# Second layer norm of a transformer block: statistics at the residual sum, rows read back in exchanged 32-blocks and turned by VectorE

## The chip, the cores and the metric

The kernel runs on one core of a Trainium2 chip. The metric is the device time of one execution in microseconds, given as the median of several runs. Engines are named as the profile names them: PE is TensorE (PEld its weight loads), DVE is VectorE, ACT is ScalarE, POOL is GpSimd, SP is SyncE, which here only issues DMA transfers.

## The reference

One block over 2048 tokens of 1024 features, in float32: layer norm, linear attention with a learned feature map (32 heads of 32), residual; then layer norm, an MLP with relu (1024 to 3584 to 1024), residual.

```python
def _layernorm(x, eps=1e-5):
    m, v = mean(x, -1), var(x, -1)
    return (x - m) / sqrt(v + eps)

# attention: q, k, v = x @ wqkv, per head
phi_q = concat(softmax(q @ w_phi), softmax(-(q @ w_phi)));  phi_k likewise
o = phi_q @ (phi_k.T @ v) / (phi_q @ phi_k.sum(0) + 1e-6)
h = x + attention(layernorm(x)) @ wo
out = h + relu(layernorm(h) @ w1) @ w2
```

The change concerns `layernorm(h)`, the second layer norm. TensorE needs its result with the features on the partitions, while `h` has the tokens there.

## The kernel before

There are 16 row tiles of 128 tokens (`NT`, half of them `HT` = 8). Every float32 product is made of three products of split operands (`mm3`, lines 181 to 183): a rounded high part and the remainder. A split is a cast on ScalarE (L124 for weights) and a subtraction on VectorE or GpSimd (L128).

The stages follow each other on TensorE: projections to keys, values and queries; attention and its output projection (`wo`) interleaved, tile group by tile group; the up projection; the down projection. Up and down are products of 2x2 blocks by seven multiplications (Winograd's form of Strassen), so the normalised rows are needed as seven sums of blocks, `hs[b, m]`, for each half `b` of the tokens.

The order is written out by hand. `items` is the list of pieces of TensorE work; each item of 8 steps (4 in the up projection) has three matmuls a step. `when(step, f, ...)` hangs other work behind a step. The instructions of each engine are issued in that order, and each engine works through its own queue in order. Steps below are counted in this unit. The class `Units` loads weight tiles (`raw`, six buffers) and splits them into a ring of ten (`w`), as soon as a place is free and the step allows. All its loads go through SP's queue, as do nearly all other transfers.

The path of the second layer norm before the change:

- `wo_load` (L645) reads the tile of x, `wo_add` (L671) adds it to the projection in PSUM on VectorE, `wo_store` (L674) writes the sum to DRAM as `hd[t]`.
- `ln_pair(b, i, stage)` takes two row tiles, one of each half of the rows of `b`: stage 0 reads both back (L214, 512 KB each), stage 1 takes statistics on VectorE (L220, L222), stage 2 makes scale and shift on GpSimd (L229 to L231), stage 3 normalises on ScalarE (L237, 128x1024), stages 4 to 6 turn three halves by TensorE (four transposes each into a PSUM bank, L244) and evict them on ScalarE (L246), stage 7 turns the last half (L701; for `b` = 0 evicted by ScalarE, L703) and forms two sums on VectorE (L705, L706), stage 8 forms two more on GpSimd (L711, L712).
- `ln_store` (L721) writes the seven blocks to `hs`, `h_load` (L729) reads them for the up projection, `h_high` and `h_low` (L737, L741) split them.

`LN2` gives the steps of the stages. The four pairs of `b` = 0 run beside attention and `wo`, 40 steps apart; the four of `b` = 1 run beside the up projection of `b` = 0, 68 steps apart. Beside the first run the attention steps of unit `u`: `at_load` (L530, a read of 512 KB through SP), `at_sums` (L562, GpSimd), `at_reduce`, `at_den`, `at_inverse`, `at_scale` (L600, GpSimd), `at_turn` (L606, VectorE, turns 32x32 blocks in place) and `at_num` (L620, TensorE), whose banks are evicted to `oT` by ScalarE (L627) and VectorE (L638). The up projection's blocks are evicted by `up_take` (L764) and the other functions of `UP_BESIDE`.

Of the kernel before, what the change touches and what calls it, by code (L numbers as in the profile page):

```python
# [15 lines left out]
P = 128  # L16
# [123 lines left out]
def kernel(  # L140
# [56 lines left out]
    hd = [dram.tile([P, D], F32, name=f"hd{t}") for t in range(NT)]  # L197

# [26 lines left out]
    def ln_power(key):  # L225

        mv = xst[key]
        sc = scx[:, key[1] - HT, :] if key[0] == "s" else lnp.tile([P, 2], F32, name="sc", bufs=4)
        pool.tensor_scalar_add(sc[:, 0:1], mv[:, 1:2], LN_EPS)  # L229
        pool.tensor_tensor(out=sc[:, 0:1], in0=sc[:, 0:1], in1=half, op=ALU.pow)  # L230
        pool.tensor_scalar(sc[:, 1:2], mv[:, 0:1], sc[:, 0:1], -1.0, op0=ALU.mult, op1=ALU.mult)  # L231
        xst[key] = sc

    def ln_norm(key):
        sc, src = xst.pop(("s", key[1]) if key[0] == "x" and key[1] >= HT else key), xin.pop(key)
        xnt[key] = src if key[0] == "h" else fp_ln.tile([P, D], F32, name="xn")
        act.activation(xnt[key], src, AF.Identity, bias=sc[:, 1:2], scale=sc[:, 0:1])  # L237

    def ln_turn(key, j, dst=None):
# [5 lines left out]
        if dst is None:  # L245
            act.activation(xn[:, j * 512:(j + 1) * 512], pt.rearrange("p k n -> p (k n)"), AF.Copy)  # L246
            return
# [430 lines left out]

    def ln_pair(b, i, stage):

        keys = [("h", HT * b + 4 * r + i) for r in range(2)]
        if stage == 0:
            for key in keys:
                ln_load(key, [hd[key[1]]])
        elif stage == 1:
            for key in keys:
                ln_stats(key)
        elif stage == 2:
            for key in keys:
                ln_power(key)  # L690
        elif stage == 3:
            for key in keys:
                ln_norm(key)
        elif stage in (4, 5, 6):
            ln_turn(keys[stage // 6], stage != 4)
        elif stage == 7:
            x1, x2 = (xnt[key] for key in keys)
            s12 = (mp or hp).tile([P, 2, 512], F32, name="s12", bufs=1)
            pt = tp_bank()
            for k in range(4):  # L700
                pe.transpose(pt[:, k * P:(k + 1) * P], x2[:, k * P:(k + 1) * P], ident)  # L701
            if b == 0:
                act.activation(s12[:, 1, :], pt, AF.Copy)  # L703
                pt = s12[:, 1, :]
            v.tensor_add(s12[:, 0, :], pt, x2[:, 512:])  # L705
            v.tensor_sub(x2[:, 0:512], x1[:, 0:512], pt)  # L706
            sums[b, i] = s12
        elif stage == 8:
            x1, s12 = xnt[keys[0]], sums[b, i]
            s4 = (mp or hp).tile([P, 512], F32, name="s4l", bufs=1)  # L710
            pool.tensor_tensor(out=s12[:, 1, :], in0=s12[:, 0, :], in1=x1[:, 0:512], op=ALU.subtract)  # L711
            pool.tensor_tensor(out=s4, in0=x1[:, 512:], in1=s12[:, 1, :], op=ALU.subtract)  # L712
            sums[b, i] = s12, s4
# [322 lines left out]
    for (t, hf), n in order:  # L1036
        do(max(n - 1, wo_first), -1, wo_load, t, hf)
        when(8 * n + (11 if n < wo_first + 2 else 9), wo_add, t, hf)
# [4 lines left out]
    LN2 = ((0, 9, 12, 17, 24, 25, 26, 27, 29, 36), (0, 18, 26, 32, 40, 42, 44, 46, 50, 60))  # L1043
    wo0 = 8 * wo_first
    up0 = 8 * first_up
    for i in range(4):
        for stage in range(9):
            when(wo0 + 64 + 40 * i + LN2[0][stage], ln_pair, 0, i, stage)
            when(up0 + 60 + 68 * i + LN2[1][stage], ln_pair, 1, i, stage)
        for j in range(7):  # L1050
            when(wo0 + 64 + 40 * i + LN2[0][9] + j // 2, ln_store, 0, i, j)
            when(up0 + 60 + 68 * i + LN2[1][9] + j, ln_store, 1, i, j)
# [56 lines left out]
    scx = consts.tile([P, HT, 2], F32, name="scx")  # L1109
    consts.tile([P, 48], F32, name="fill")  # L1110
# [94 lines left out]
```

## Time and profile before

| | before |
|---|---|
| median of 3 runs | 1911.11 us (1909.57 to 1911.47) |
| span of the profiled execution | 1907.8 us |
| the profiled execution's own time | not listed apart from the runs; its span is 3.3 us below their median |
| VectorE busy | 1034.8 us (54%) |
| ScalarE busy | 758.0 us (40%) |
| GpSimd busy | 974.2 us (51%) |
| granted TensorE clock | 0.999 |
| DMA | 432.14 MB, mean 227 GB/s |

A row of groups gives line, engine, operation, tiles, shapes and count, then the busy time in us and the mean duration in ns, then the idle time of the engine just before and what ended it. A row of the timeline gives start, length, engine and line. A row of a table by stretches gives the bounds in us, the length, then the busy time of PE, PEld, DVE, ACT and POOL with the instructions, the granted clock, the DMA share and GB/s. A row of DMA issues gives the count, the size, and the median time from issue to landing in us.

### The profile page before, as it was taken

The page shows a single profiled execution, that of the slowest core. Times are in us where ns is not written, and L with a number is a line of the kernel's source. Part 1 is how long each engine was busy: PE and PEld are TensorE (multiplying, and loading weights), DVE is VectorE, ACT ScalarE, POOL GpSimd, SP SyncE. Part 2 cuts the span into 40 slices and gives each one's busy share as a digit, 9 for nine tenths or more (in the row PEclk, how much of TensorE's full clock was granted, in tenths as well). Part 3 has the DMA queues.
Part 4 walks back from the last instruction along what each step waited for, and adds up shares of the span by engine and source line. Part 5 has one row for each costly group of instructions (what it writes and reads, how often), then busy time and mean ns, then how long its engine had stood idle before and what let it go on. Part 6 is the DMA issues. An engine that isn't in the chain of part 4 may idle for free.

```text
span 1907.8 us, 31460 instructions
## 1 busy us (share of the span) xinstructions
PE 1894.3 (99%) x11416; PEld 1561.0 (82%) x11416; DVE 1034.8 (54%) x1657; ACT 758.0 (40%) x1314; POOL 974.2 (51%) x961
## 2 busy tenths in 40 slices
PE   9999999999999999999999999999999999999999
PEld 7888888877878888878888888888888888888887
DVE  6666578767679876545644564344433433343333
ACT  5433326222223222245445564444444444444442
POOL 4777752789955988523333222222244444444443
PEclk9999999999999999999999999999999999999999
DMA  6888786666665667796786897566677677767775
GB/s 225 274 267 269 233 273 196 212 192 210 201 196 195 216 206 242 216 303 219 256 252 229 276 294 220 175 195 191 205 255 222 192 239 234 240 212 221 215 215 177
DMA packets 292699, 432.14 MB, mean 227 GB/s; under 512 B 24384, under 2 KB 150336, under 8 KB 292544
## 3 DMA queue, kind: packets, MB, share of 16 engines
q1 hardware_dynamic: 275648, 413.36, 68.5%
q10 hardware_dynamic: 16896, 16.78, 2.6%
q8 instruction: 89, 1.46, 0.3%
q14 instruction: 66, 0.54, 0.1%
HBM read 292.68 MB, written 137.36 MB: 225 GB/s over the span
## 4 chain that ended last, share of the span: by engine, by line
PE 88%; POOL 5%; DMA 4%; issue 1%; DVE 1%; SPq 1%; ACT 0%; POOLq 0%; DVEq 0%; ACTq 0%
PE mm L181 22%; PE mm L182 22%; PE mm L183 22%; PE ac L181 4%; PE ac L182 4%; PE ac L183 4%; PE tp L182 2%; PE tp L183 2%; PE tp L181 2%; POOL b L350 2%; POOL w L128 2%; PE tp L244 1%; PE tp L278 1%; DMA b<-in_w_dram 1%; DMA t<-b 1%
## 5 line engine op out<-in xcount | busy, mean ns | idle before, releaser
L128 POOL TENSOR_TENSOR w<-raw,w 128x512 fp32r<-128x512 f32 x355 | 474.5, 1338 | 725.6 <-ACT w L124 683.2
L124 ACT ACTIVATE w<-raw 128x512 fp32r<-128x512 f32 x686 | 409.3, 626 | 510.8 <-PE mm L183 247.4
L128 DVE TENSOR_TENSOR w<-raw,w 128x512 fp32r<-128x512 f32 x331 | 270.3, 817 | 531.1 <-ACT w L124 527.9
L181 PE MATMUL mm<-w,xT 128*128 128x512 f32 x768 | 311.9, 406 | 0.0
L182 PE MATMUL mm<-w,xT 128*128 128x512 f32 x768 | 301.0, 392 | 3.3 <-POOL w L128 2.9
L183 PE MATMUL mm<-w,xT 128*128 128x512 f32 x768 | 300.6, 391 | 0.0
L182 PE MATMUL mm<-hT,w 128*128 128x512 f32 x672 | 261.7, 389 | 1.3 <-DVE hT L741 1.3
L181 PE MATMUL mm<-hT,w 128*128 128x512 f32 x672 | 262.7, 391 | 0.0
L183 PE MATMUL mm<-hT,w 128*128 128x512 f32 x672 | 261.7, 389 | 0.0
L350 POOL TENSOR_TENSOR b<-b 128x256 f32<-128x256 f32 x224 | 181.9, 812 | 89.7 <-DMA b<-in_w_dram 74.2
L182 PEld LDWEIGHTS mm<-w,xT 128*128 128x128 f32 x768 | 145.0, 189 | 33.6 <-POOL w L128 5.1
L181 PEld LDWEIGHTS mm<-w,xT 128*128 128x128 f32 x768 | 144.9, 189 | 30.8 <-issue 1.7
L183 PEld LDWEIGHTS mm<-w,xT 128*128 128x128 f32 x768 | 144.5, 188 | 30.9
L183 PE MATMUL mm<-w 128*128 128x512 f32 x392 | 152.6, 389 | 0.0
L182 PE MATMUL mm<-w 128*128 128x512 f32 x392 | 152.6, 389 | 0.0
L181 PE MATMUL mm<-w 128*128 128x512 f32 x392 | 152.5, 389 | 0.0
L182 PEld LDWEIGHTS mm<-hT,w 128*128 128x128 f32 x672 | 126.2, 188 | 27.4 <-DVE hT L741 1.7
L183 PEld LDWEIGHTS mm<-hT,w 128*128 128x128 f32 x672 | 126.1, 188 | 26.4
L181 PEld LDWEIGHTS mm<-hT,w 128*128 128x128 f32 x672 | 126.2, 188 | 25.8
L182 PEld LDWEIGHTS mm<-w 128*128 128x128 f32 x392 | 73.6, 188 | 15.3
L183 PEld LDWEIGHTS mm<-w 128*128 128x128 f32 x392 | 73.6, 188 | 15.2
L181 PEld LDWEIGHTS mm<-w 128*128 128x128 f32 x392 | 73.6, 188 | 15.3
(164 smaller groups left out, 3148.6 us busy)
## 6 DMA issues: line engine op xcount, KB each, us to landing
raw<-t SPq DMA_DIRECT2D x224, 256.0 KB, 4.0
raw<-ad SPq DMA_DIRECT2D x196, 256.0 KB, 3.0
raw<-in_w_dram SPq DMA_DIRECT2D x168, 256.0 KB, 3.1
b<-in_w_dram SPq DMA_DIRECT2D x56, 512.0 KB, 4.2
t<-b SPq DMA_DIRECT2D x56, 512.0 KB, 4.2
ad<-c SPq DMA_DIRECT2D x112, 256.0 KB, 3.7
ad<-s SPq DMA_DIRECT2D x84, 256.0 KB, 4.1
ed<-qe ACTq DMA_DIRECT2D x32, 512.0 KB, 4.9
```

The costliest lines, as they stand in the source:

```text
L124: nc.scalar.activation(w[:, 0, :], raw[1], AF.Copy)
L128: eng.tensor_tensor(out=w[:, 1, :], in0=raw[1], in1=w[:, 0, :].bitcast(F32), op=ALU.subtract)
L181: pe.matmul(ps, a_hi, b_hi, start=first, stop=False, skip_group_check=more)
L182: pe.matmul(ps, a_hi, b_lo, start=False, stop=False, skip_group_check=more)
L183: pe.matmul(ps, a_lo, b_hi, start=False, stop=last, skip_group_check=more)
L244: pe.transpose(pt[:, k, :], xn[:, (4 * j + k) * P:(4 * j + k + 1) * P], ident)
L278: pe.matmul(ps[:, i * P:(i + 1) * P], wt_of[p, i][:, k * P:(k + 1) * P], bd[:, (2 * p + i) % 8, :], start=True, stop=True)
L350: pool.tensor_tensor(out=tsum[j, *out], in0=tsum[j, *a], in1=tsum[j, *b], op=ALU.subtract)
```

## The change

The statistics are taken by VectorE right after the residual sum, from the sum in SBUF. GpSimd makes scale and shift there, and SP writes them to a small DRAM array `scd[t]` (8 bytes a row). The tile is read back from `hd` in four transfers (one for each 32 destination partitions), in runs of 32 elements, so that each 32 columns of features come to stand where a 32x32 block turn needs them; with each goes a transfer that reads the scales of the same exchanged rows into `scx`. ScalarE normalises in four passes a tile, one for each group of 32 rows (scale and shift differ between them). VectorE turns the 32x32 blocks in place, and the sums follow from SBUF. TensorE's transposes for this layer norm and their evictions are gone, and the steps in `LN2` are new. The first layer norm keeps its transposes.

```diff
--- before.py
+++ after.py
@@ -195,6 +195,7 @@
     place_of = {t: (b, i) for b, tiles in enumerate(groups) for i, t in enumerate(tiles)}
     ed = [dram.tile([P, 8, 4, 256], F32, name=f"ed{b}") for b in range(4)]
     hd = [dram.tile([P, D], F32, name=f"hd{t}") for t in range(NT)]
+    scd = [dram.tile([P, 2], F32, name=f"scd{t}") for t in range(NT)]
 
 
 
@@ -225,7 +226,7 @@
     def ln_power(key):
 
         mv = xst[key]
-        sc = scx[:, key[1] - HT, :] if key[0] == "s" else lnp.tile([P, 2], F32, name="sc", bufs=4)
+        sc = scx[:, key[1] - HT, 0, :] if key[0] == "s" else lnp.tile([P, 2], F32, name="sc", bufs=4)
         pool.tensor_scalar_add(sc[:, 0:1], mv[:, 1:2], LN_EPS)
         pool.tensor_tensor(out=sc[:, 0:1], in0=sc[:, 0:1], in1=half, op=ALU.pow)
         pool.tensor_scalar(sc[:, 1:2], mv[:, 0:1], sc[:, 0:1], -1.0, op0=ALU.mult, op1=ALU.mult)
@@ -233,18 +234,15 @@
 
     def ln_norm(key):
         sc, src = xst.pop(("s", key[1]) if key[0] == "x" and key[1] >= HT else key), xin.pop(key)
-        xnt[key] = src if key[0] == "h" else fp_ln.tile([P, D], F32, name="xn")
+        xnt[key] = fp_ln.tile([P, D], F32, name="xn")
         act.activation(xnt[key], src, AF.Identity, bias=sc[:, 1:2], scale=sc[:, 0:1])
 
-    def ln_turn(key, j, dst=None):
+    def ln_turn(key, j, dst):
 
         xn = xnt[key]
         pt = tp_bank().rearrange("p (k n) -> p k n", k=4)
         for k in range(4):
             pe.transpose(pt[:, k, :], xn[:, (4 * j + k) * P:(4 * j + k + 1) * P], ident)
-        if dst is None:
-            act.activation(xn[:, j * 512:(j + 1) * 512], pt.rearrange("p k n -> p (k n)"), AF.Copy)
-            return
         d = dst()
         split(d[:, 0, 4 * j:4 * j + 4, :], d[:, 1, 4 * j:4 * j + 4, :], pt)
         if j == 1:
@@ -676,37 +674,46 @@
 
 
 
+    def wo_stats(t, hf):
+        if hf == 0:
+            hst[t] = lnp.tile([P, 2, 6], F32, name="st", bufs=4)
+        v.bn_stats(out=hst[t][:, hf, :], in_=xh[t, hf])
+        if hf == 1:
+            xst["h", t] = mv = lnp.tile([P, 2], F32, name="mv", bufs=4)
+            v.bn_aggr(out=mv, in_=hst.pop(t))
+
+    hst = {}
+
+    def wo_scale(t):
+        sp.dma_start(scd[t], xst.pop(("h", t)))
+
     def ln_pair(b, i, stage):
 
-        keys = [("h", HT * b + 4 * r + i) for r in range(2)]
+        tiles = [HT * b + 4 * r + i for r in range(2)]
         if stage == 0:
-            for key in keys:
-                ln_load(key, [hd[key[1]]])
+            for r, t in enumerate(tiles):
+                xnt["h", t] = x = lnp.tile([P, D], F32, name="xin")
+                for a in range(4):
+                    rows = slice(32 * a, 32 * (a + 1))
+                    sp.dma_start(scx[rows, 2 * i + r], scd[t].rearrange("(g t) s -> t g s", g=4))
+                    sp.dma_start(x[rows].rearrange("p (c g k) -> p c g k", c=8, g=4),
+                                 hd[t].rearrange("(g t) (c a k) -> a t c g k", g=4, a=4, k=32)[a])
         elif stage == 1:
-            for key in keys:
-                ln_stats(key)
-        elif stage == 2:
-            for key in keys:
-                ln_power(key)
-        elif stage == 3:
-            for key in keys:
-                ln_norm(key)
-        elif stage in (4, 5, 6):
-            ln_turn(keys[stage // 6], stage != 4)
-        elif stage == 7:
-            x1, x2 = (xnt[key] for key in keys)
-            s12 = (mp or hp).tile([P, 2, 512], F32, name="s12", bufs=1)
-            pt = tp_bank()
-            for k in range(4):
-                pe.transpose(pt[:, k * P:(k + 1) * P], x2[:, k * P:(k + 1) * P], ident)
-            if b == 0:
-                act.activation(s12[:, 1, :], pt, AF.Copy)
-                pt = s12[:, 1, :]
-            v.tensor_add(s12[:, 0, :], pt, x2[:, 512:])
-            v.tensor_sub(x2[:, 0:512], x1[:, 0:512], pt)
-            sums[b, i] = s12
-        elif stage == 8:
-            x1, s12 = xnt[keys[0]], sums[b, i]
+            for r, t in enumerate(tiles):
+                x = xnt["h", t].rearrange("p (c g k) -> p c g k", c=8, g=4)
+                for g in range(4):
+                    sc = scx[:, 2 * i + r, g]
+                    act.activation(x[:, :, g], x[:, :, g], AF.Identity, bias=sc[:, 1:2], scale=sc[:, 0:1])
+        elif stage in (2, 3):
+            x = xnt["h", tiles[stage - 2]]
+            v.transpose(x, x)
+        elif stage == 4:
+            x1, x2 = (xnt["h", t] for t in tiles)
+            sums[b, i] = s12 = (mp or hp).tile([P, 2, 512], F32, name="s12", bufs=1)
+            v.tensor_add(s12[:, 0, :], x2[:, 0:512], x2[:, 512:])
+            v.tensor_sub(x2[:, 0:512], x1[:, 0:512], x2[:, 0:512])
+        elif stage == 5:
+            x1, s12 = xnt["h", tiles[0]], sums[b, i]
             s4 = (mp or hp).tile([P, 512], F32, name="s4l", bufs=1)
             pool.tensor_tensor(out=s12[:, 1, :], in0=s12[:, 0, :], in1=x1[:, 0:512], op=ALU.subtract)
             pool.tensor_tensor(out=s4, in0=x1[:, 512:], in1=s12[:, 1, :], op=ALU.subtract)
@@ -1035,21 +1042,26 @@
     order = sorted(wo_n.items(), key=lambda kv: kv[1])
     for (t, hf), n in order:
         do(max(n - 1, wo_first), -1, wo_load, t, hf)
-        when(8 * n + (11 if n < wo_first + 2 else 9), wo_add, t, hf)
+        added = 8 * n + (11 if n < wo_first + 2 else 9)
+        when(added, wo_add, t, hf)
+        when(added, wo_stats, t, hf)
+        if hf == 1:
+            when(added + 2, ln_power, ("h", t))
+            when(added + 5, wo_scale, t)
         when(8 * n + (10 if n > order[-3][1] else 14), wo_store, t, hf)
 
 
 
-    LN2 = ((0, 9, 12, 17, 24, 25, 26, 27, 29, 36), (0, 18, 26, 32, 40, 42, 44, 46, 50, 60))
+    LN2 = ((5, 14, 18, 20, 22, 24, 30), (0, 14, 20, 24, 28, 32, 42))
     wo0 = 8 * wo_first
     up0 = 8 * first_up
     for i in range(4):
-        for stage in range(9):
+        for stage in range(6):
             when(wo0 + 64 + 40 * i + LN2[0][stage], ln_pair, 0, i, stage)
             when(up0 + 60 + 68 * i + LN2[1][stage], ln_pair, 1, i, stage)
         for j in range(7):
-            when(wo0 + 64 + 40 * i + LN2[0][9] + j // 2, ln_store, 0, i, j)
-            when(up0 + 60 + 68 * i + LN2[1][9] + j, ln_store, 1, i, j)
+            when(wo0 + 64 + 40 * i + LN2[0][6] + j // 2, ln_store, 0, i, j)
+            when(up0 + 60 + 68 * i + LN2[1][6] + j, ln_store, 1, i, j)
     assert wo_n[8, 0] + 10 < first_up
 
     def up_step(b, p, m):
@@ -1106,8 +1118,7 @@
     eps = consts.tile([P, 1], F32, name="eps")
     pool.memset(eps, DEN_EPS / 2)
     act.activation(consts.tile([P, 1], F32, name="first"), half, AF.Exp)
-    scx = consts.tile([P, HT, 2], F32, name="scx")
-    consts.tile([P, 48], F32, name="fill")
+    scx = consts.tile([P, HT, 4, 2], F32, name="scx")
     wphi = fp.tile([P, 8, 32], F32, name="wphi", bufs=1)
     sp.dma_start(wphi, w_phi.rearrange("(j i) e f -> i e j f", i=4))
     ln_load(("x", 0), [x[0:P, 0:512], x[0:P, 512:1024]])
```

## The prediction

> **What bounds the kernel now.** I read first the page's busy times and the shares of the chain that ended last.
>
> ```profile
> span 1907.8 us, 31460 instructions
> ...
> PE 1894.3 (99%) x11416; PEld 1561.0 (82%) x11416; DVE 1034.8 (54%) x1657; ACT 758.0 (40%) x1314; POOL 974.2 (51%) x961
> ...
> PE 88%; POOL 5%; DMA 4%; issue 1%; DVE 1%; SPq 1%; ACT 0%; POOLq 0%; DVEq 0%; ACTq 0%
> ```
>
> TensorE is busy for 1894.3 of 1907.8 us, so 13.5 us idle is all there is over the whole span. Work taken off TensorE shortens the span unless something makes TensorE wait instead. The median of three runs, 1911.11 us, is 3.3 us above the span of the profiled execution. I sum against the span and add 3.3.
>
> Next come the groups of instructions, for what the change removes, and TensorE's timeline around one pair of row tiles (start, length, engine, line), for what it really costs.
>
> ```profile
> L244 PE MATMUL tp<-ident,xin 128*128 128x128 f32 x96 | 14.4, 273 | 0.0
> L701 PE MATMUL tp<-ident,xin 128*128 128x128 f32 x32 | 4.8, 272 | 0.0
> ```
>
> ```profile
> 692.01 0.39 PE L183 MATMUL mm<-w,oT 128*128 128x512 f32 x1
> 692.24 0.39 PE L181 MATMUL mm<-w,oT 128*128 128x512 f32 x1
> 692.46 0.39 PE L182 MATMUL mm<-w,oT 128*128 128x512 f32 x1
> 692.69 0.39 PE L183 MATMUL mm<-w,oT 128*128 128x512 f32 x1
> 692.92 0.60 PE L244 MATMUL tp<-ident,xin 128*128 128x128 f32 x4
> 693.28 0.48 PE L181 MATMUL mm<-w,oT 128*128 128x512 f32 x1
> 693.59 0.40 PE L182 MATMUL mm<-w,oT 128*128 128x512 f32 x1
> 693.83 0.39 PE L183 MATMUL mm<-w,oT 128*128 128x512 f32 x1
> ...
> 697.21 0.40 PE L183 MATMUL mm<-w,oT 128*128 128x512 f32 x1
> ```
>
> The durations overlap, so neither 273 ns nor the group's busy time is the price. The starts give it. Three matmuls without transposes take 692.69 - 692.01 = 0.68 us, which is one step of the hand-written order. With four transposes among them they take 693.83 - 692.69 = 1.14. From 692.69 to 697.21 lie four such stretches (three of L244, one of L701), 1.13 us each. Four transposes therefore cost 1.13 - 0.68 = 0.45 us.
>
> **The change part by part.**
>
> *TensorE.* Of each of eight pairs 16 transposes go, 96 + 32 = 128 in all, in 32 groups of four: 32 x 0.45 = 14.4 us off an engine that never waits at these places. This is the only large gain. The higher bound would be the groups' busy time, 14.4 + 4.8 = 19.2 us; I take the starts, because the neighbours' overlap is in them.
>
> *ScalarE, VectorE, GpSimd.* ScalarE loses per tile one 128x1024 pass (1.24 us) and per pair three or four 128x512 evictions (0.60 each), and gets eight 128x256 passes (no row of SBUF to SBUF at that size; half of 1.24 at most). So it is no busier. VectorE gets 16 turns of 128x1024 at 1.21 us by the row below, two a pair; its statistics (two of 0.68 us a tile) only move ahead, to behind the residual sum. GpSimd's three small operations a tile move ahead too.
>
> ```profile
> L237 ACT ACTIVATE xin<-xin,sc 128x1024 f32<-128x1024 f32 x16 | 19.5, 1238 | 15.7 <-POOL sc L231 15.4
> L246 ACT ACTIVATE xin<-tp 128x512 f32<-128x512 f32 x24 | 14.4, 598 | 19.9 <-PE tp L244 19.7
> L606 DVE STREAM_TRANSPOSE xin<-xin 128x1024 f32<-128x1024 f32 x4 | 4.8, 1208 | 0.0
> L220 DVE BATCH_NORM_STATS2 st<-xin 128x6 f32<-128x512 f32 x64 | 40.7, 677 | 13.5 <-DMA xin<-in_x_dram 7.9 <-DMA xin<-hd 5.5
> ```
>
> In all VectorE gains 16 x 1.21 = 19.3 us spread over the span, at 54% busy. I cost this at nothing; its cover is that idle half, and if it is gone it shows as attention work late for TensorE (below).
>
> *The read-back.* Two loads of 512 KB a pair become eight of 128 KB in runs of 128 bytes, with eight tiny loads of the scale between them and one tiny store a tile: 16 issues where there were two. Only one transfer of the old kernel has such runs, the first load of all: 128 KB in 1024 runs of 128 bytes.
>
> ```profile
> qe<-ed SPq DMA_DIRECT2D x28, 512.0 KB, 5.4
> ...
> xin<-hd SPq DMA_DIRECT2D x16, 512.0 KB, 5.4
> ...
> wphi<-in_w_phi_dram SPq DMA_DIRECT2D x1, 128.0 KB, 2.5
> ```
>
> ```profile
> 0.72 0.44 SPq L1112 DMA_DIRECT2D wphi<-in_w_phi_dram  x1
> 1.22 1.04 SPq L214 DMA_DIRECT2D xin<-in_x_dram  x2
> ```
>
> ```profile
> 1.80:2.00 0.20, 0.20 (x2) 0.20 (x3) 0.12 (x1) 0.20 (x1) 0.00 (x0) 1.00 0.47 80
> 2.00:2.20 0.20, 0.20 (x3) 0.20 (x3) 0.00 (x0) 0.19 (x1) 0.00 (x0) 1.00 1.08 173
> ```
>
> It lands 2.5 us after its issue, and in the stretch 2.00 to 2.20 us the queues move 173 GB/s (last column), when the next load, issued half a microsecond later, has hardly begun. At 173 GB/s a load of 131 KB takes 0.76 us, and eight take 6.1 us. The other end counts the whole 2.5 us as transfer, one behind the other: 8 x 2.5 = 20 us. I take a value near the first, since the second puts the latency of one load into all eight. SP issues at 0.44 us each: 16 x 0.44 = 7.0 us. In the built order each transfer of SP also waits for the one eight places before it, but 8 x 0.44 = 3.5 us exceeds the 2.5 us landing. So SP is held for about 7 us, and the last tile stands about 7.0 + 2.5 = 9.5 us after the first issue (20 us at the bad end).
>
> Here the Trainium skill speaks against the change: "DMA: Bandwidth & Descriptors", Rules for kernel authors, says that a plain DMA with a rearranged access pattern is 19 times slower than a transposing one. That gives a rival below; the landing of 2.5 us does not bear it out.
>
> *Who waits behind that.* SP's queue also carries weight loads, attention's reads of exponentials (L530) and the reads of x. Weights are asked for many steps ahead; the ring holds ten units, 40 steps in the up projection, 40 x 0.68 = 27 us, so 7 us is covered. The attention reads are not. In steps counted from the same origin, the loads of the first four pairs stand at 157, 197, 237 and 277, the attention reads at 151, 167, 183, 199 and so on by 16. Only the second pair's set stands right ahead of one (197, 199). The old timeline at that place, SP, GpSimd, VectorE and TensorE:
>
> ```profile
> 714.43 0.42 SPq L674 DMA_DIRECT2D hd<-xh  x1
> 714.96 1.82 SPq L530 DMA_DIRECT2D qe<-ed  x2
> ```
>
> ```profile
> 708.45 5.02 POOL L562 TENSOR_TENSOR ez<-qe,zb 128x512 f32<-128x512 f32 x4
> ...
> 722.03 5.02 POOL L562 TENSOR_TENSOR ez<-qe,zb 128x512 f32<-128x512 f32 x4
> ```
>
> ```profile
> 734.19 2.36 DVE L606 STREAM_TRANSPOSE qe<-qe 128x1024 f32<-128x1024 f32 x2
> ```
>
> ```profile
> 739.74 0.34 PE L620 MATMUL tp<-qe,kvL 32*32 32x128 f32 x8
> ```
>
> The read is issued at 714.96, lands by the median 5.4 us later, 720.4, and is used at 722.03: 1.6 us of slack. The turned result is there at 734.19 + 2.36 = 736.55, and TensorE wants it at 739.74: 3.2 us more. A read late by 7 to 8 us makes TensorE wait 7.8 - 1.6 - 3.2 = 3 us, once.
>
> *ScalarE waiting for the tiles.* The first four pairs normalise 9 steps after their loads (a step there, with attention between, is 0.85 us: L562 stands 16 steps apart, 722.03 - 708.45 = 13.6 us), so 7.6 us; the later four 14 steps after, 14 x 0.68 = 9.5 us. Against 9.5 us the second tile of a pair is late by at most 2 us, the time in which the first is normalised. Behind the wait on ScalarE stand weight casts (27 us ahead) and the evictions of the up projection. The one with the least room is the block that the next group opens, 4 steps or 2.7 us on; by the step counts only the eighth pair's normalisation falls just before it. I take 1 us there. VectorE waits likewise at its turns, 4 steps after; it is covered by the 3.2 us.
>
> *From attention to the MLP.* The queues are near full there, and TensorE has its one wait for this layer norm's output:
>
> ```profile
> L182 PE MATMUL mm<-hT,w 128*128 128x512 f32 x672 | 261.7, 389 | 1.3 <-DVE hT L741 1.3
> ```
>
> ```profile
> 806.00:830.00 24.00, 24.00 (x108) 19.87 (x107) 11.78 (x12) 6.31 (x9) 6.75 (x5) 1.00 0.96 307
> ...
> 850.00:866.00 16.00, 14.72 (x65) 11.84 (x64) 13.28 (x15) 10.45 (x17) 4.71 (x3) 1.00 0.77 224
> ```
>
> The DMA share (second column from the right) is 0.96, and TensorE is busy 14.72 of 16.00 us. The fourth pair's stores stand 6 steps earlier than before, which can remove these 1.3 us; 16 more issues and four small stores that wait for GpSimd can as well double them. I take a loss of 1 us, from -1.3 to +3.
>
> Sum: 1907.8 - 14.4 + 3 + 1 + 1 = 1898.4 us span, and 3.3 more: 1901.7 us.
>
> **The rivals.**
>
> *Short runs are slow, and the kernel is slower.* If each 128 KB load takes its 2.5 us in full, a pair needs 20 us. Then ScalarE, and VectorE and GpSimd behind it, stand 20 - 7.6 = 12.4 us in each of three pairs beside attention; with 1.6 + 3.2 of slack TensorE loses 7.6 us each, 23 us. In the later four it is 20 - 9.5 = 10.5 us against 12 steps or 8.2 us of slack at most evictions, 2.3 us each, 9 us. 1911.1 - 14.4 + 23 + 9 + 1 = 1930 us. It decides from where the losses pass 14.4 us: about 16 us a pair, or 2 us a load. For it: no row shows 128-byte runs under load, with 32 partitions as the target. Against: 173 GB/s.
> At the old rate (307 GB/s at share 0.96, 320 at 1.00) a pair's 1.05 MB takes 3.3 us; 19 times that is 62 us, of which by the same sums (62 - 7.6 - 4.8) x 3 + (62 - 9.5 - 8.2) x 4 = 326 us would reach TensorE: about 2220 us. That is the skill's rule taken whole; I give it 2 in 100.
>
> *The waits cascade, and nothing is gained.* The load set is fast enough, but its holds meet attention's chain over GpSimd (28.67 of 30 us busy between 690 and 720), which has no time to make them up:
>
> ```profile
> 690.00:720.00 30.00, 30.00 (x380) 24.50 (x379) 21.34 (x37) 5.77 (x13) 28.67 (x33) 1.00 0.70 223
> ```
>
> Then 3 us are lost in three pairs, 1.5 in each of the later four and 1 between, 16 us in all: 1912.7, no change.
>
> *No hold reaches TensorE.* Then 14.4 us are gained and at best the 1.3 us wait also: 1895.4 to 1896.7.
>
> That the transposes stay is excluded: the built order has 128 fewer matmuls on TensorE and no other difference there in kinds and counts.
>
> **How the numbers follow.** The forecast with its small losses has 0.65 (own range 1897 to 1907), no hold at all 0.10, the cascade 0.10, slow runs 0.13, the rule of 19 times 0.02. What a measurement of this kernel can tell from no change is 0.2%, 3.8 us: faster is under 1907.3, slower over 1914.9. The cascade falls two fifths to faster or slower, three fifths to same; with the forecast's and the rival's edges that gives faster 0.78, same 0.07, slower 0.15. The range runs from 1895, all gained, to 1916, the beginning of the slow rival.
>
> **What would show it.** Right: TensorE's busy time near 1880 us; 0.68 us between L183's at all places where transposes were; the 128 KB loads landing in 2.5 to 4 us; SP held about 7 us a pair; one wait of TensorE for L620 of about 3 us near 740 us. Wrong: landings over 6 us, ScalarE idle for the tiles for more than 5 us a pair, or TensorE's idle time grown by over 10 us.

## The result: 2.7% slower

| | before | after |
|---|---|---|
| median | 1911.29 us (4 runs, 1909.57 to 1911.73) | 1963.88 us (4 runs, 1962.21 to 1965.98) |
| ratio, 95% interval | | 1.0269 [1.0255, 1.0283] |
| span of the profiled execution | 1907.8 us | 1963.5 us |
| granted TensorE clock | 0.999 | 0.985 |

The forecast was 1901.7 us, in a range from 1895 to 1916. The time came out 62 us above it, outside the range and on the other side of before. The page of the changed kernel, lines as shown for before (span; busy time, share and count by engine; shares of the chain that ended last):

```profile
span 1963.5 us, 31404 instructions
PE 1902.4 (97%) x11288; PEld 1559.5 (79%) x11288; DVE 1058.3 (54%) x1673; ACT 754.0 (38%) x1334; POOL 969.6 (49%) x961
PE 46%; issue 0%; DVE 0%; ACT 0%
```

128 matmuls are gone, and yet TensorE is busy 1902.4 us, longer than the 1894.3 of before, and idle 61.1 us where it was idle 13.5. The idle time says that TensorE now waits; the busy time, that the same matmuls ran slower. The bytes are as before (432.22 MB against 432.14). The chain followed back covers only 46% of the span here, so the place of the loss has to be read by stage.

The yardstick is the experiment e1 below, which has the same work on TensorE as the changed kernel, the same steps and statistics, and the old plain reads: 1894.82 us. The two kernels by stretches (bounds and length in us; busy time of PE, PEld, DVE, ACT, POOL; granted clock; DMA share; GB/s). The first stretch begins at 600 us in both, where the two still stand within a few matmuls of each other; the other bounds are the same points of the program: the last start of attention's products (L618), the first matmul of the up projection on `hT`, the last one, and the end. First the changed kernel, then e1:

```profile
600.00:808.40 208.40, 187.78 (x2438) 149.26 (x2443) 153.41 (x259) 40.33 (x95) 157.32 (x195) 0.93 0.70 178
808.40:862.00 53.60, 45.18 (x223) 36.49 (x209) 23.71 (x29) 13.81 (x24) 11.07 (x12) 0.94 0.96 220
862.00:1425.60 563.60, 544.26 (x2349) 447.10 (x2350) 267.53 (x338) 265.34 (x449) 152.31 (x117) 0.98 0.76 225
1425.60:1963.50 537.90, 534.00 (x2356) 441.82 (x2355) 191.13 (x255) 222.44 (x384) 248.79 (x192) 1.00 0.72 220
```

```profile
600.00:778.10 178.10, 175.76 (x2432) 141.01 (x2436) 153.03 (x257) 39.60 (x94) 157.81 (x194) 1.00 0.66 218
778.10:822.70 44.60, 44.60 (x222) 36.82 (x206) 30.16 (x40) 18.08 (x29) 19.26 (x21) 1.00 0.93 298
822.70:1355.20 532.50, 532.50 (x2351) 441.14 (x2351) 257.28 (x328) 261.96 (x443) 145.52 (x108) 1.00 0.74 232
1355.20:1893.10 537.90, 533.94 (x2356) 442.04 (x2354) 191.65 (x255) 222.92 (x384) 248.78 (x192) 1.00 0.73 220
```

Beside attention the changed kernel loses 30.3 us, between attention and the up projection 9.0, in the up projection 31.1, and in the down projection, where none of this runs, nothing. In each stretch both parts are there: length less busy time, and busy time against e1's. Beside attention 18.3 us are more idle and 12.0 more busy, at a granted clock of 0.93 against 1.00. What TensorE waits for in the changed kernel (in all, times, longest, us):

```profile
PE tp L618 <- DVE qe L604: 12.0, 3, 6.3
PE mm L181 <- ACT hT L744: 11.1, 2, 8.3
PE mm L181 <- DVE c L774: 6.3, 2, 4.2
PE mm L183 <- DVE oT L636: 5.7, 2, 5.1
PE mm L181 <- DVE xh L669: 4.8, 1, 4.8
```

L618, L604 and L636 are attention's products, turns and evictions (L620, L606 and L638 before), L744 the split of the up projection's input, L669 the residual sum, L774 an eviction of the up projection. Two stops of the up projection's stretch:

```profile
877.70 0.79 PE L181 MATMUL mm<-hT,w 128*128 128x512 f32 x1 [4.77 <-DVE xh L669]
...
995.88 0.69 PE L181 MATMUL mm<-hT,w 128*128 128x512 f32 x1 [4.16 <-DVE c L774]
```

The first belongs to the start of the stage, which the late fourth pair and the late residual sums hold up. By matmul counts at e1's pace about 18 of the 31.1 us are lost there, before the first read-back of this stage begins at 923.8 us. The second stands beside the stage's second pair, read from 974.46 to 986.92 us, and its way is another than beside attention:

```profile
984.27 2.08 ACT L706 ACTIVATE xin<-xin,scx 128x256 f32<-128x256 f32 x4 [4.77 <-DMA scx<-scd]
992.80 0.69 DVE L128 TENSOR_TENSOR w<-raw,w 128x512 fp32r<-128x512 f32 x1 [13.96 <-ACT w L124]
```

ScalarE, which works in order, stands for the scales of the first tile and again (3.81 us) ahead of the second. The weight cast behind these passes comes late, VectorE stands 13.96 us for it, and the eviction that TensorE needs stands behind that on VectorE.

The stops beside attention are for nothing that the layer norm makes: attention's own chain has come late. (The turns and sums of the layer norm can lengthen it: ahead of the eviction L636 that ends the stop at 750.89 below, VectorE waits 5.99 us for GpSimd's L560 and then spends 3.8 us on them.) The timeline shows how, around the second pair. SP first (start, length):

```profile
719.83 0.44 SPq L698 DMA_DIRECT2D scx<-scd  x1
720.32 0.56 SPq L699 DMA_DIRECT2D xin<-hd  x1
720.93 0.67 SPq L698 DMA_DIRECT2D scx<-scd  x1
...
730.76 0.56 SPq L699 DMA_DIRECT2D xin<-hd  x1
731.42 0.62 SPq L688 DMA_DIRECT2D scd<-sc  x1
...
732.61 2.36 SPq L528 DMA_DIRECT2D qe<-ed  x2
...
739.31 0.33 SPq L643 DMA_DIRECT2D xh<-in_x_dram  x1
747.38 0.32 SPq L688 DMA_DIRECT2D scd<-sc  x1
...
748.27 0.88 SPq L528 DMA_DIRECT2D qe<-ed  x2
```

and GpSimd in the same stretch (in brackets how long it was idle just before, and for what):

```profile
741.00 5.03 POOL L560 TENSOR_TENSOR ez<-qe,zb 128x512 f32<-128x512 f32 x4 [6.17 <-DMA qe<-ed]
...
747.09 0.26 POOL L232 TENSOR_SCALAR sc<-mv,sc 128x1 f32<-128x1 f32 x1
```

The sixteen issues hold SP from 719.83 to 731.32, and attention's read L528, queued behind them and a scale store, goes out at 732.61. GpSimd stands 6.17 us for it. Behind that stand the three small operations that make the scale of the next row tile; they end at 747.35. SP has stood since 739.64 at the store of that scale (L688), which it issues at 747.38; the next attention read is behind it, at 748.27. So the delay goes round: SP late, GpSimd late, SP late. The same in sums, the changed kernel first, then e1, which has neither the sixteen issues nor the stores. (`qtz`, L576, is GpSimd's operation right behind the last of the three; the store itself reads `sc`, so its two rows belong together.)

```profile
POOL ez L560 <- DMA qe<-ed: 32.9, 8, 11.7
SPq L688 <- POOL qtz L576: 31.6, 4, 10.6
SPq L688 <- POOL sc L232: 14.2, 4, 7.7
```

```profile
POOL ez L560 <- DMA qe<-ed: 1.6, 4, 0.6
SPq L528 <- POOL qtz L576: 0.4, 2, 0.3
```

And after its longer stops TensorE runs slower for a while:

```profile
745.22 0.39 PE L181 MATMUL mm<-w,oT 128*128 128x512 f32 x1
745.45 0.39 PE L182 MATMUL mm<-w,oT 128*128 128x512 f32 x1
750.89 0.80 PE L183 MATMUL mm<-w,oT 128*128 128x512 f32 x1 [5.05 <-DVE oT L636]
751.48 0.63 PE L181 MATMUL mm<-w,oT 128*128 128x512 f32 x1
751.91 0.63 PE L182 MATMUL mm<-w,oT 128*128 128x512 f32 x1
...
757.29 0.39 PE L183 MATMUL mm<-w,oT 128*128 128x512 f32 x1
```

Before the stop matmuls start 0.23 us apart, after it 0.43, for 6.4 us, until 757.29. The Trainium skill, "TensorE: Matmul & The Clock Gate", Part 1, says that an idle window of about 3.4 us halves the clock and that about as long a busy one restores it. The trace agrees on the size (0.43 against 0.23); here the slow stretch lasted 6.4 us.

### The profile page after: what moved, and what is told of

The parts are those of the page before. It is cut to its first block, busy times and chain, and to the rows that moved or that the text cites. A ratio compares the mean times of both kernels' runs of the same rounds, so it can differ in the third digit from the quotient of the medians.

```text
span 1963.5 us, 31404 instructions
## 1 busy us (share of the span) xinstructions
PE 1902.4 (97%) x11288; PEld 1559.5 (79%) x11288; DVE 1058.3 (54%) x1673; ACT 754.0 (38%) x1334; POOL 969.6 (49%) x961
## 2 busy tenths in 40 slices
DMA packets 368475, 432.22 MB, mean 220 GB/s; under 512 B 102208, under 2 KB 228160, under 8 KB 368320
## 5 line engine op out<-in xcount | busy, mean ns | idle before, releaser
L128 DVE TENSOR_TENSOR w<-raw,w 128x512 fp32r<-128x512 f32 x331 | 274.9, 831 | 545.2 <-ACT w L124 537.3
L181 PE MATMUL mm<-hT,w 128*128 128x512 f32 x672 | 266.2, 396 | 24.4 <-ACT hT L744 11.1
L182 PE MATMUL mm<-hT,w 128*128 128x512 f32 x672 | 265.5, 395 | 3.2 <-DVE hT L748 3.2
L183 PE MATMUL mm<-hT,w 128*128 128x512 f32 x672 | 264.7, 394 | 0.0
L181 PEld LDWEIGHTS mm<-hT,w 128*128 128x128 f32 x672 | 128.4, 191 | 54.3 <-ACT hT L744 11.9
L182 PEld LDWEIGHTS mm<-hT,w 128*128 128x128 f32 x672 | 128.3, 191 | 31.0 <-DVE hT L748 4.2
L183 PEld LDWEIGHTS mm<-hT,w 128*128 128x128 f32 x672 | 128.4, 191 | 26.9
L183 PEld LDWEIGHTS mm<-w 128*128 128x128 f32 x392 | 73.6, 188 | 15.3
L182 PEld LDWEIGHTS mm<-w 128*128 128x128 f32 x392 | 73.6, 188 | 15.3
```

The costliest lines, as they stand in the source:

```text
L128: eng.tensor_tensor(out=w[:, 1, :], in0=raw[1], in1=w[:, 0, :].bitcast(F32), op=ALU.subtract)
L181: pe.matmul(ps, a_hi, b_hi, start=first, stop=False, skip_group_check=more)
L182: pe.matmul(ps, a_hi, b_lo, start=False, stop=False, skip_group_check=more)
L183: pe.matmul(ps, a_lo, b_hi, start=False, stop=last, skip_group_check=more)
```

## Experiments

The theory to begin with: the transposes are worth what was forecast, and the transfers eat it, by their number, since SP issues them in order with attention's reads. Rivals: the short runs themselves are slow; the statistics and turns, or the new steps, hurt; the stores that wait for GpSimd hurt. Times are medians; ratios, with their 95% interval, are against the kernel before on the same chip. e2, e13, e14, e16 and e17 have eight to twelve runs each, the others two, so differences of a few us between the latter are not firm. In the code cuts `...` stands for what is left out.

### Which part of the read-back costs

**e1: one plain read a tile, no exchange, no scale transfers** (scales straight from SBUF).

```diff
-  for a in range(4):
-      sp.dma_start(scx[rows, 2 * i + r], scd[t]...)
-      sp.dma_start(x[rows]..., hd[t]...[a])
+  sp.dma_start(x, hd[t])
```

> The change without the exchange: each tile is read back by one transfer of whole rows, and scale and shift come straight from SBUF (so rows and scales are not exchanged, and the output leaves the exchange out). Two issues a pair, no scale stores; VectorE's turns, ScalarE's four passes and the missing TensorE transposes stay. Theory S (SP's queue is the loss: 16 issues of 0.56 and 0.67 us hold it 11 to 15 us a pair, attention's reads stand behind): 1895 to 1902 us. Theory D (the 128-byte runs are the loss): the same. Rival V (the work moved to VectorE and ScalarE, turns of 1.24 us and eight passes of 0.59 us a pair, is the loss): over 1940 us.

1894.82 us, 0.9915 [0.9886, 0.9944]. TensorE is busy 1878.5 us, 15.8 less than before, and idle 14.6. That is what the removal is worth, about 17 us by the medians (11 to 22 by the interval), with the statistics moved, VectorE's turns and ScalarE's four passes all in place. None of these is the cause.

**e2: the eight exchanged reads, without scale transfers and stores.**

```diff
-      sp.dma_start(scx[rows, 2 * i + r], scd[t]...)
...
-        sp.dma_start(scd[t], xst.pop(("h", t)))
```

> The exchanged read stays (eight transfers a pair in 128-byte runs), the scale stores and the eight scale reads are left out; scale and shift come from SBUF in the unexchanged rows. Theory S: SP is held 8 x 0.6 = 5 us a pair, most of the loss goes: 1898 to 1915 us. Theory D: all the short runs are still there: over 1940 us.

1907.33 us, 0.9972 [0.996, 0.9983]: 12.5 us over e1, and 56.6 under the changed kernel. SP's timeline at the first pair, of e2 and then of e1:

```profile
674.03 10.46 SPq L698 DMA_DIRECT2D xin<-hd  x8
```

```profile
674.53 0.90 SPq L696 DMA_DIRECT2D xin<-hd  x2
```

Eight issues take 10.46 us, 1.3 us each. So the short runs do hold SP, here as long as sixteen issues at their shortest in the changed kernel (10.43 us); but over eight pairs the hold, from the first issue to the end of the last, is 9.6 us on average against 13.1 in the changed kernel, while the cost is 12.5 us against 69. The hold alone does not set the cost.

**e3: sixteen issues and the stores, but each tile read takes whole rows.**

```diff
-  sp.dma_start(x[rows].rearrange(...), hd[t].rearrange(...)[a])
+  sp.dma_start(x[rows], hd[t][rows])
```

> All 16 issues a pair and the scale stores stay, but each tile transfer reads 32 whole rows (4 KB runs) instead of 128-byte runs, so the exchange is left out. Theory S: the issues and their order are the same, the hold stays 8 to 11 us: 1935 to 1965 us. Theory D: 1897 to 1910 us.

1939.56 us, 1.0149 [1.012, 1.0179]: without short runs of tile data 44.7 us over e1 remain. SP waits for GpSimd as in the changed kernel (29.7 us for `qtz`).

**e7: the kernel before, with fourteen unused reads of 1 KB ahead of each pair's two.**

```diff
+  for a in range(7):
+      rows = slice(32 * (a % 4), 32 * (a % 4 + 1))
+      sp.dma_start(dum[rows], x[key[1] * P:(key[1] + 1) * P, 0:2].rearrange("(g t) s -> t g s", g=4))
   ln_load(key, [hd[key[1]]])
```

> The kernel before, TensorE transposes and all, with seven small reads (1 KB, 128 runs of 8 bytes, nobody uses them) ahead of each of the two tile reads of a pair: 16 issues a pair where there were two. Theory S: SP is held 10 us a pair, attention's reads and the weights come late as after the change: 1930 to 1960 us. Theory D, and a theory W that the scale stores waiting for GpSimd are the loss: 1911 to 1916 us, the bytes are next to none and nothing waits for GpSimd.

1943.61 us, 1.017 [1.0141, 1.02]: 31.5 us for transfers that move nothing to speak of and that nobody waits for, in the old kernel. TensorE's longest wait, and SP's issues for the first tile of the second pair:

```profile
PE tp L244 <- ACT xin L237: 11.2, 3, 6.2
```

```profile
717.64 6.05 SPq L686 DMA_DIRECT2D dum<-in_x_dram  x7
```

So fourteen more small transfers a pair in SP's queue are enough to cost tens of us. The way is another here: the tile reads themselves came last, and GpSimd's wait for attention's reads stays at 1.0 us.

**e13: the statistics alone moved; scales stay in SBUF, reads and transposes as before.**

```diff
+  elif stage in (1, 2):
+      pass
...
+  when(added, wo_stats, t, hf)
+  if hf == 1:
+      when(added + 2, ln_power, ("h", t))
```

> The kernel before with one part of the change alone: statistics and scales are made at the residual sum, the scales stay in SBUF in row order; reading back, TensorE's transposes and the sums are as before. Theory S/T (the gain of the run with plain reads, 17 us, is TensorE's transposes, the loss is the read-back): 1908 to 1912 us, no change. Rival M (the moved statistics gave part of that gain, because VectorE no longer holds for the tiles): 1903 to 1907 us.

1914.66 us, 1.0014 [1.0005, 1.0024]. Early statistics bring nothing by themselves (they cost 3 us, if anything); so the gain of e1 belongs to the transposes, with their evictions.

### The stores, and the place in the queue

**e4: the scale stores 15 steps later** (3 for tile 4), behind the GpSimd work that makes the scales.

```diff
-  when(added + 5, wo_scale, t)
+  when(added + (8 if t == 4 else 20), wo_scale, t)
```

**e5: the sixteen issues spread over 15 steps**, the later stages 8 to 10 steps later beside attention and 4 to 8 beside the up projection. **e6: both.**

```diff
+  for m in range(8):
+      when(wo0 + 64 + 40 * i + LN2[0][0] + 2 * m, ln_pair, 0, i, -1 - m)
...
-  LN2 = ((5, 14, 18, 20, 22, 24, 30), (0, 14, 20, 24, 28, 32, 42))
+  LN2 = ((5, 24, 27, 29, 31, 33, 38), (0, 22, 26, 30, 34, 38, 46))
```

> The full change with one difference: the stores of the scales stand 15 steps later in SP's order (3 for the first tile that is read back), so that GpSimd has long made them when SP comes to them. Theory W (SP stuck at the scale stores behind GpSimd, 46 us of waits in the changed kernel, is a main part of the loss): 1915 to 1940 us. Theory S alone (the 16 issues of the read-back): little goes, 1945 to 1965 us.

> The full change, but the 16 issues of a pair's read-back are spread over 15 steps, two at a time, with the other work of SP between them; normalising, turns, sums and stores stand 8 to 10 steps later accordingly. The same number of issues, bytes and runs. Theory S (it is the hold in one piece that delays what stands behind): 1900 to 1925 us. If SP's total time were short, and not the hold in one piece, it would stay at 1945 to 1965 us. Theory W: the scale stores still wait, so some 20 to 30 us stay.

> The read-back spread over 15 steps and the scale stores moved 15 steps later, both. If S and W together are the loss: 1896 to 1905 us, faster than the kernel before. If the issues cost SP time that it does not have between attention and the MLP in any order: 1910 to 1930 us.

e4 1947.82 us, 1.0193 [1.0138, 1.0248]; e5 1968.27, 1.03 [1.027, 1.033]; e6 1947.64, 1.0192 [1.0153, 1.0231]. The later stores give back 16 us (two runs, 1943.7 and 1952.0, so the size is rough), and the 31.6 us of SP's wait for `qtz` are 1.1 in e4:

```profile
SPq L688 <- POOL qtz L576: 1.1, 1, 1.1
```

That half of the circle is shown. By the stretches it belongs to attention: e4 gets back 10.8 us there and 1.6 in the up projection. The other half stays, and spreading does not help it; e5 is slower than any forecast for it. In e5 and e6 the issues of a pair take 14 to 29 us on SP. Other reads may then come late a little each, not much once, which is not shown; and the stages moved later run into the next stretch, so the test is not clean.

**e15: e2 spread in the same way**, to see spreading without scales; its edit of e2 is e5's of the changed kernel.

> The run without scales (1907 us: eight tile reads a pair in 128-byte runs, scale and shift in the unexchanged rows) with its eight reads spread over 15 steps and the later stages 8 to 10 steps later. The 12.5 us between that run and plain reads (1895 us) are then either the hold in one piece: 1895 to 1900 us, or the short runs' load on the queues in any order (theory D in part): 1904 to 1910 us.

1925.89 us, 1.0074 [1.0052, 1.0097]: 18.6 us worse than e2. One wait shows the later stages' part in it:

```profile
PE mm L181 <- DMA hs<-xin: 5.6, 1, 5.6
```

**e8: e6 with the scales of a pair in one array, read together** (twelve issues a pair).

```diff
-  sp.dma_start(scx[rows, 2 * i + r], scd[t]...)
+  if r == 0:
+      sp.dma_start(scx[rows, 2 * i:2 * i + 2]..., scd[b, i]...)
```

> As the run with both, and the scales of the two tiles of a pair lie side by side in DRAM, so that one transfer reads both: four scale reads a pair instead of eight, 12 issues in all. Theory S: 4 x 0.67 = 2.7 us of SP's time less a pair; if SP's time still cost something after the spreading, 3 to 10 us faster than that run, else the same within 3 us.

1929.52 us, 1.0097 [1.0068, 1.0126]: four of sixteen reads fewer give 18 us against e6. The bytes are the same, but the runs of 8 bytes have become half as many runs of 16, so this does not tell a transfer's count from that of its runs.

### Another queue

**e9: e6 with the scales' reads and stores issued by ScalarE. e10: all sixteen and the stores. e12: e8 with the scales by ScalarE. e11: the changed kernel with attention's reads by ScalarE.**

```diff
-  sp.dma_start(scx[rows, ...], scd...); sp.dma_start(scd..., ...)
+  act.dma_start(scx[rows, ...], scd...); act.dma_start(scd..., ...)
...
-  sp.dma_start(x[rows]..., hd[t]...[a])
+  act.dma_start(x[rows]..., hd[t]...[a])
...
-  sp.dma_start(e..., ed[u // 8][:, u % 8])
+  act.dma_start(e..., ed[u // 8][:, u % 8])
```

The first edit is that of e9 and e12, the first two that of e10, the third that of e11.

> As the run with spread read-back and late scale stores (1948 us), but the scale reads and scale stores are issued from ScalarE's queue; SP keeps the eight tile reads a pair. Theory S, now as SP's time in all (spreading did nothing, fewer issues did): SP has the load of the run without scales (1907 us), ScalarE gives some 6 us a pair of its idle time: 1900 to 1915 us. If instead the transfers themselves, their landing or the eight completion counters they share with SP's, are the limit, the queue does not matter: 1940 to 1955 us.

> All 16 issues of a pair's read-back and the scale stores from ScalarE's queue. Theory S: SP is as free as before the change: 1896 to 1905 us, unless ScalarE, held 10 us a pair, makes casts and evictions late: then 1910 to 1935 us. Rival (completion counters, landing): 1940 to 1955 us.

> As the run with the scales on ScalarE's queue, and with the scales of a pair read together (four scale reads a pair instead of eight). Theory S: ScalarE is held 2.7 us a pair less: the same as that run or up to 8 us faster, 1896 to 1910 us. Rival: as the paired run on SP, 1925 to 1935 us.

> The full change as it is, with one difference: attention's reads of the exponentials are issued from ScalarE's queue, so that they no longer stand behind SP's read-back. Theory S says of the loss of 67 us that about 30 us arise up to the last attention matmul and 37 us behind it: the first part goes, the second (blocks of the normalised rows and weights late at the up projection) stays: 1930 to 1945 us. If attention's reads were not the way in which SP's lateness reaches TensorE: 1955 to 1970 us.

e9 1950.24 us, 1.02 [1.017, 1.0229]; e10 1953.43, 1.0216 [1.0185, 1.0248]; e12 1932.99, 1.011 [1.0081, 1.014]; e11 1957.14, 1.0236 [1.0203, 1.0268]. Only e11 is below its partner on SP, the changed kernel, by 7 us with intervals that overlap; by the theory it was to be 19 to 34. GpSimd still waits 27.5 us for attention's reads there, which now stand on ScalarE behind passes that wait 27.2 us for `scx`. The others have 1.02, 1.0216 and 1.011 where e6, e6 and e8 have 1.0192, 1.0192 and 1.0097, as the rival in their forecasts had it: the queue does not matter. So it is too narrow to say that SP's time is the cost. ScalarE's queue is in order as well; e10's evictions of attention stand behind it:

```profile
741.11 0.66 ACT L625 ACTIVATE oT<-tp 128x256 fp32r<-128x256 f32 x2 [20.78 <-DMA xin<-hd]
```

Nor was SP set free. The issues of both queues share eight completion counters (what a transfer raises when it has landed), and in e10 SP waits for ScalarE's transfers, whose data its weight loads (L324) and stores (L672) do not need:

```profile
SPq L672 <- DMA xin<-hd: 13.7, 5, 5.0
SPq L324 <- DMA scx<-scd: 10.5, 6, 6.7
```

So the counters tie the two queues together; how much of e10's loss goes by them and how much by ScalarE's own order was not separated.

### Other ways to the same layout

**e14: pairs beside attention as before; pairs beside the up projection exchanged**, with paired scales and reads spread over 21 steps.

```diff
-  when(wo0 + 64 + 40 * i + LN2[0][stage], ln_pair, 0, i, stage)
+  when(wo0 + 64 + 40 * i + LN2[0][stage], ln_pair_old, 0, i, stage)
...
+  for m in range(8):
+      when(up0 + 60 + 68 * i + LN2[1][0] + 3 * m, ln_pair, 1, i, -1 - m)
```

> A version meant to beat both: the four pairs beside attention as before the change, the four pairs beside the up projection as after it, their scales read for both tiles together (12 issues a pair) and spread over 21 steps, normalising 29 steps after the first read. Gain 4 x 16 transposes = 16 groups of four x 0.45 = 7.2 us. If the loss beside the up projection was only the lateness of ScalarE's and VectorE's work, it goes with the wider spacing: 1903 to 1906 us. If the extra transfers reach TensorE there in any order: 1908 to 1920 us.

1914.65 us, 1.0015 [1.0006, 1.0023]. Half of the transposes are gone, worth 7.2 us by the forecast's price, and nothing of it is left even there, where no attention reads are in the queue: the stretch from the first up matmul on `hT` to the last is 542.8 us, against 541.6 before and 532.5 in e1. Part of this may be the moved statistics, since e13 has the same median (its stretch is 545.9).

**e16: the changed kernel's whole result, with the scales exchanged by one small product a pair on TensorE** (128x128 by 128x16, with a 0/1 matrix) in place of the scale transfers. **e17: the same, beside attention the second pair 3 steps later and the third 2 earlier**, so that their reads do not stand right ahead of an attention read.

```diff
-  sp.dma_start(scx[rows, 2 * i + r], scd[t]...)
+  pool.tensor_tensor(out=rx[:, 4 * r:4 * r + 4, :], in0=sc[:, None, :].to_broadcast([P, 4, 2]),
+                     in1=ident[:, 0:4, None].to_broadcast([P, 4, 2]), op=ALU.mult)
...
+  pe.matmul(ps[:, 0:16]..., ones, rx, start=True, stop=True)
...
+  act.activation(scx[:, :, 0, :], sel_ps.pop((b, i))[:, 0:16]..., AF.Copy)
```

```diff
-  when(wo0 + 64 + 40 * i + LN2[0][stage], ln_pair, 0, i, stage)
+  when(wo0 + 64 + 40 * i + (0, 3, -2, 0)[i] + LN2[0][stage], ln_pair, 0, i, stage)
```

> The change with its scale transfers replaced: scale and shift stay in SBUF, GpSimd lays each tile's pair of columns into the four columns of its row group (two small operations a tile more in all), and one small TensorE product a pair (128x128 by 128x16) exchanges them; so the full result with eight transfers a pair, the steps otherwise as after the change. If the transfers of the scales were the main loss (theory S in its refined form): as the run without scales, 1907 us, and 8 products of at most 0.5 us: 1905 to 1913 us. If the run without scales was fast for another reason: over 1930 us.

> The run before it, with the second pair beside attention 3 steps later (so that attention's read is issued ahead of its eight tile reads, not behind) and the third 2 steps earlier. The remaining 12.5 us over plain reads are by the trace of the run without scales mostly one stop of TensorE there, 5.8 us and the lower clock behind it. If the place in SP's queue is what does it: 1897 to 1904 us, faster than the kernel before. If the short runs cost wherever they stand: 1905 to 1912 us.

e16 1910.09 us, 0.9997 [0.9988, 1.0007]; e17 1911.81, 1.0007 [0.9998, 1.0016]. With no transfer for the scales the loss of 2.7% is gone. (`ones` and four columns of `ident` are filled with the 0/1 pattern once, ahead of attention's output projection; the row has two matmuls a product.) The page of e16 and the price of the product:

```profile
span 1902.8 us, 31338 instructions
PE 1882.3 (99%) x11304; PEld 1547.9 (81%) x11304; DVE 1057.2 (56%) x1677; ACT 754.4 (40%) x1342; POOL 976.7 (51%) x977
...
L698 PE MATMUL tp<-scx,ones 128*128 128x16 f32 x16 | 2.3, 220 | 0.0
```

53.8 us come back for 2.3 us of TensorE. They come back in both stretches, 26.8 us beside attention and 25.5 in the up projection; so the scale transfers are the cause of most of the loss in both. In the up projection it is not the stores' wait, since e4 gets back only 1.6 us there. What remains against e1 is 15.3 us, near e2's 12.5: the eight exchanged reads. For the two pairs that e17 moves, their place in the queue was not it. No version with the whole result beat the kernel before; e1's 1894.8 us, which leaves the exchange out, marks what the idea could bring with these steps.

## Why the prediction was wrong

- *TensorE, 14.4 us*: right, a little low. e1 measures 15.8 us of busy time, and about 17 us in the median.
- *ScalarE, VectorE, GpSimd at nothing*: right as long as attention's chain is on time. VectorE gained 23.5 us of busy time (1034.8 to 1058.3; 19.3 forecast), ScalarE lost 4.0, and e1 pays for neither.
- *The landing of the 128 KB reads, 2.5 to 4 us*: right.

```profile
qe<-ed SPq DMA_DIRECT2D x28, 512.0 KB, 7.1
xin<-hd SPq DMA_DIRECT2D x64, 128.0 KB, 3.4
scx<-scd SPq DMA_DIRECT2D x64, 1.0 KB, 3.1
scd<-sc SPq DMA_DIRECT2D x16, 1.0 KB, 6.1
```

  The rival of 19 times is out. The factor of 19 that the Trainium skill gives for a rearranged plain transfer ("DMA: Bandwidth & Descriptors", Rules for kernel authors) does not show at this run length: 3.4 us here against 5.4 for plain reads four times as large. But landing alone was the wrong thing to ask of short runs. They hold SP in issue (e2).
- *SP held for 7.0 us a pair*: **the first step that failed.** It took 0.44 us from the one such transfer, which was issued alone. In a row the issues go 0.56 and 0.67 us long, an issue pair every 1.32 us, with stalls: 10.4 to 15.8 us a pair, 13.1 on average. The hold alone is not the loss (e2 has 9.6 us and loses little); what stands behind it made it one.
- *Only the second pair's set stands right ahead of an attention read*: failed with it. The first and third sets stand ten steps, 8.5 us, ahead of the next one; that was enough for 7 us and is not for the 15.8 and 14.9 that they took. GpSimd waited eight times, not once.
- *The scale stores at nothing beside attention*: **the second.** What is queued behind was asked of the reads, and not of the store, which waits in SP's queue for GpSimd (45.8 us of SP's time in the two rows of L688 above); e4 prices it at roughly 16 us.
- *3 us once for L620* (L618 after the change): 12.0 us in three stops, and the chain behind them reaches the up projection. *From attention to the MLP, 1 us*: 9.0. *ScalarE waiting for the tiles, 1 us*: **the third**, by the same hold. With 7.0 + 2.5 us the last tile was to be there at the 9.5 us of lead; a set of 12.5 us and 3.1 more to land is not. ScalarE waits 28.5 us for `scx` in seven stops (18.6 us of it ahead of the up projection), the longest 10.2, with weight casts and evictions behind it, and the up projection's stretch loses 31.1, at its start and beside its first pairs.
- *A stop costs its length*: nowhere said, and assumed throughout. 70.4 us of span over e1 are 46.5 of idle time and 23.9 of slower matmuls, half as much again.
- *The cascade*, with 0.10 and 16 us, was the right mechanism with the right cover gone (GpSimd without time to make it up). Its size was taken from the forecast's 3 us a pair, and it had no way back from GpSimd to SP. *Short runs are slow* foresaw the sign and a term that is real (12.5 us, e2), about a fifth of the whole, though by landing, which was not slow. (By its own terms the losses pass 14.4 us at about 17 us a pair, not 16.)

What stays open: how e2's 12.5 us divide between SP's hold and the data's own way, why spreading is worse, whether the scale transfers cost by their number or by their 128 runs of 8 bytes each, and how much the shared counters cost where ScalarE issues.

## What to carry to other kernels

Count a transfer by its issue, in the shape and the run of issues it will have, and by what waits behind it in its queue; here 128 KB and 1 KB in short runs held SP about equally long in a mixed row (0.56 and 0.67 us), and sixteen reads and two stores a pair in place of two reads cost 69 us. Never put a store that waits for an engine into an in-order queue ahead of a read on which that engine waits; if a few values must change partitions, try a small matmul: here it was far cheaper than the transfers. Price a stop of TensorE above its length, and test a layout change first with the transfer left plain, which tells what the idea is worth without it.

## What the hardware showed that was not expected

- Issue time depends on shape and on neighbours: 0.32 to 0.45 us for the first scale read of most sets, 0.67 for most of those behind it, 0.56 for a 128 KB read in 128-byte runs between them, and 0.9 to 1.4 us a read for eight such reads in a row (e2), against 0.45 us for a plain read of 512 KB (e1, two in 0.90).
- Transfers that move 1 KB each and that nobody uses made the old kernel 1.7% slower (e7).
- Transfers issued by ScalarE held SP as well: SP waited 13.7 and 10.5 us for their landing, with no data in common (e10).
- After a stop of 5.05 us matmuls ran at 0.43 us in place of 0.23 for another 6.4 us.
